# Attention and expert layers on one core: crossbar transposes issued one row further ahead, result stores moved to ScalarE's queue, and a re-ordered start

## The chip, the cores and the metric

The kernel runs on one core of a Trainium2 chip. The metric is the device time in microseconds (us) of one launch. Three runs of the kernel before gave a median of 343.33 us (342.6 to 345.01). Three later sets of rounds gave it medians of 344.21, 345.04 and 346.3 us, so a variant is always compared with runs of the kernel before on the same chip and in the same rounds.

## The reference

Attention with two kinds of heads, followed by a layer of two matrix products with a squared ReLU between:

```python
# q, k, v: (8, 8, 576, 64): batch rows, heads, positions, head size
scores = (q @ k.transpose(0, 1, 3, 2)) / sqrt(64)
rel = pos[:, None] - pos[None, :]
# heads 0..3 ("sliding"): 0 <= rel < 32
# heads 4..7 ("dilated"): 0 <= rel < 128 and rel % 4 == 0
attn = softmax(where(mask, scores, -1e9))
x = (attn @ v).transpose(0, 2, 1, 3).reshape(4608, 512)
h = x @ moe_w_in                 # 512 x 2048
g = maximum(h, 0) ** 2
out = g @ moe_w_out              # 2048 x 512, float32 out
```

## The kernel before

The 4608 tokens are cut in nine chunks of 512. The expert layer of a chunk is 64 matmuls into `ph` (with ReLU on ScalarE and the square on VectorE), then 64 into `po`, each result copied by ScalarE and stored. These are generators. `pump(n)` lets n "steps" of two matmuls each out, and the attention of row b is laid between the steps of chunk b-1. So "row b" and "chunk b-1" name the same stretch of time.

```python
osb   = ctx.enter_context(tc.tile_pool(name="osb", bufs=3))     # relu out and result
pmool = ctx.enter_context(tc.tile_pool(name="pmool", bufs=4, space=PSUM))
# single buffers: QKTp, QKTd (transposed q and k), AT, vp, vd (cast v),
#                 sv, sd (v as loaded), sq (q and k as loaded)

def load_sliding_v(b):               # six DMAs on SP, the sync engine
    for m in range(NB):
        ...
        nc.sync.dma_start(out=sv[p0:P, m, :, :], in_=...)

def load_v(b):
    load_sliding_v(b)
    load_dilated_v(b, nc.sync)       # two more, into sd

def keep_sliding_qk(b, n):           # q, k cast to f16, written to HBM (dd: those of the dilated heads)
    d = dpool.tile([2, S, HH * D], FP16, name=f"dp{b}", tag="dp")
    for i in (1, 0):
        nc.sync.dma_start(out=d[i]..., in_=n[:, i]...)
    return d

def transpose_by_dma(dp, dd):        # the crossbar transposes, T(b) below
    for i in (1, 0):
        nc.sync.dma_start_transpose(out=QKTp[:, i, :, PADP:], in_=dp[i])
        nc.sync.dma_start_transpose(out=QKTd[:, i, :, KPAD:], in_=dd[i])

def store(c, t, po):
    ot = osb.tile([P, DM], FP32, name=f"ot{c}_{t}", tag="ot")
    nc.scalar.copy(ot, po)
    nc.sync.dma_start(out=out[(c*4 + t)*P : (c*4 + t + 1)*P, :], in_=ot)

# ... row 0: on TensorE, alone; row 1: on TensorE, between the steps of chunk 0
for b in range(2, B):
    pending.append(moe_gen(b - 1))
    nq = cast_sliding_qk(b, (nc.gpsimd,) * 4)
    dp = keep_sliding_qk(b, nq)
    transpose_by_dma(dp, dd)         # T(b), for this same row
    cast_v()                         # sv, sd -> vp, vd on GpSimd
    if b + 1 < B:
        load_sliding_qk(b + 1)
        load_v(b + 1)
        dd = keep_dilated_qk(b + 1)
    pump(24)
    attn_scores(b, 4)                # needs T(b)
    attn_values(b, 2)                # needs vp, vd
    pump(1000)
```

Below, v(3) is the v load of row 3, T(3) its transposes, and so on. The "write-out" of a row is its dp.

The softmax here doesn't subtract the row's maximum and nothing guards it: scores larger than these inputs give would overflow.

Of the kernel before, what the change touches and what calls it, by code (L numbers as in the profile page):

```python
# [13 lines left out]
P = 128  # L14
# [3 lines left out]
def kernel(  # L18
# [9 lines left out]
    nc = tc.nc  # L28

    B, H, S, D = q.shape  # L30
# [58 lines left out]
    def load_sliding_qk(b, engs=(nc.sync, nc.sync)):  # L89
        for i, src in enumerate((q, k)):  # L90
            engs[i].dma_start(
                out=sq[:, i, :, :],
                in_=src[b, 0:HH].rearrange("h (p j) d -> p h (j d)", j=6),
            )
# [15 lines left out]
    def load_v(b):  # L110
        load_sliding_v(b)
        load_dilated_v(b, nc.sync)
# [8 lines left out]
                nc.gpsimd.dma_start(out=nd[48 * e : 48 * (e + 1), i, :, :], in_=s4[e])  # L121

    def load_w_in():
        for f0, f1 in ((0, 512), (512, 1024), (1024, 2048)):
            nc.gpsimd.dma_start(
                out=wi[:, :, f0:f1],
                in_=moe_w_in[:, f0:f1].rearrange("(dh dl) f -> dl dh f", dl=P),
            )
# [26 lines left out]
                )  # L155
        return n

    def cast_sliding_v():
        for m in range(0, NB, 2):
            nc.gpsimd.tensor_copy(vp[:, m : m + 2, :, 0:D], sv[:, m : m + 2, :, :])  # L160

    def cast_dilated_v():
        for t in range(2):
            for c in range(0, DIL, 2):
                nc.gpsimd.tensor_copy(  # L165
                    vd[:, t, c : c + 2, :, 0:D],
                    sd[:, t, :, D * c : D * (c + 2)].rearrange("p h (c d) -> p c h d", d=D),
                )
# [29 lines left out]
    load_sliding_qk(0, (nc.sync, nc.scalar))  # L198
    reli = const.tile([P, QB], I16, name="reli")
    nc.gpsimd.iota(reli, pattern=[[1, QB]], base=0, channel_multiplier=-1)  # L200
    make_identity(nc, ident)
    nds = {0: dilated_buffer(0)}
    load_dilated_qk(0, nds[0])
    nc.vector.memset(sv[0:PADP, 0, :, :], 0.0)
    nc.vector.memset(sd[0:64, 0, :, :], 0.0)
    load_sliding_v(0)
    load_dilated_v(0, nc.scalar)
    warm = const.tile([P, 1], FP32, name="warm")
# [63 lines left out]
    def store(c, t, po):  # L272
        ot = osb.tile([P, DM], FP32, name=f"ot{c}_{t}", tag="ot")
        nc.scalar.copy(ot, po)  # L274
        nc.sync.dma_start(out=out[(c * 4 + t) * P : (c * 4 + t + 1) * P, :], in_=ot)

    def mm2_gen(c, g):
        for t in range(TOKC // P):
# [33 lines left out]
    def pump(n):  # L312
        for _ in range(n):
            while pending:
                try:
                    next(pending[0])
                    break
                except StopIteration:
                    pending.pop(0)
# [10 lines left out]
    def t_sliding(b, n, hp, i, wide=False):  # L330
        p_ = pt(f"pt{b}_{hp}_{i}", wide)
        for j in range(6):
            nc.tensor.transpose(
                p_[:, QB * j : QB * (j + 1)],
                n[:, i, j, 2 * hp : 2 * hp + 2, :],
                ident[0:QB, 0:QB],
            )
        copy(
            nc.vector if i else nc.scalar,
            QKTp[:, i, hp, PADP:].rearrange("x (p j) -> x p j", j=6),  # L340
            p_[:, 0:UW].rearrange("x (j p) -> x p j", j=6),
        )

    def t_dilated(b, n, g, i, wide=False):
        p_ = pt(f"pd{b}_{g}_{i}", wide)
        for j in range(6):
            nc.tensor.transpose(
                p_[:, QB * j : QB * (j + 1)],
                n[:, i, g, P * j : P * (j + 1)],
                ident[0:QB, 0:QB],  # L350
            )
        for a in range(2):
            copy(
                nc.vector if i else nc.scalar,
                QKTd[:, i, a, KPAD + 2 * g * CL : KPAD + 2 * (g + 1) * CL].rearrange(
                    "x (h p s) -> x h p s", h=2, s=3
                ),
                p_[:, 0:UW].rearrange("x (s a h p) -> x a h p s", a=2, h=2, p=48)[:, a],
            )
# [5 lines left out]
    def s_sliding(b, hp):  # L365
        tiles = [pa(f"ps{b}_{hp}_{half}") for half in range(2)]
        for half, ps in enumerate(tiles):
            for m3 in range(3):
                m = 3 * half + m3
                for e in range(2):  # L370
                    r = slice(D * e, D * (e + 1))
                    nc.tensor.matmul(  # L372
                        ps[:, e, QB * m3 : QB * (m3 + 1)],
                        QKTp[r, 1, hp, QB * m : QB * m + P],
                        QKTp[r, 0, hp, PADP + QB * m : PADP + QB * (m + 1)],
                        start=True,
                        stop=True,
                    )
        for half, ps in enumerate(tiles):
            softmax(2 * hp + half, ps, maskp)  # L380
# [94 lines left out]
            py[:, 0:UW].rearrange("x (c r i) -> x c i r", c=2, r=DIL),  # L475
        )

    def transposes(b, nq, nd, gap):
        wide = gap == 0
        for hp in range(2):  # L480
            for i in (1, 0):
                t_sliding(b, nq, hp, i, wide)
                pump(gap)
        for g in range(2):
            for i in (1, 0):
                t_dilated(b, nd, g, i, wide and not i)
                pump(gap)

    def attn_scores(b, gap):
        for hp in range(2):  # L490
# [26 lines left out]


    nq = cast_sliding_qk(0, (nc.scalar, nc.scalar, nc.vector, nc.gpsimd))
    cast_sliding_v()  # L520
    load_w_in()
    cast_dilated_v()
    for hp in range(2):
        for i in (1, 0):
            t_sliding(0, nq, hp, i)
        s_sliding(0, hp)
    for g in range(2):
        for i in (1, 0):
            t_dilated(0, nds[0], g, i)
        s_dilated(0, g)  # L530
    attn_values(0, 0)


    g0 = hidden(0)
    pending.append(mm1_gen(0, g0))
    pump(6)
    nds[1] = dilated_buffer(1)
    nc.vector.memset(sq[:, :, :, 0:1], 0.0)
    nc.vector.memset(nds[1][:, :, :, 0:1], 0.0)
    load_sliding_qk(1)  # L540
    load_dilated_qk(1, nds[1])
    load_w_out()
    nq = cast_sliding_qk(1, (nc.gpsimd,) * 4)
    pump(26)
    pending.append(mm2_by_rows_gen(0, g0))
    for hp in range(2):
        for i in (1, 0):
            t_sliding(1, nq, hp, i, True)
            pump(1)
    nc.vector.memset(sv[:, 1, :, 0:1], 0.0)  # L550
    nc.vector.memset(sd[:, 1, :, 0:1], 0.0)
    load_v(1)
    cast_v()
    load_sliding_qk(2)
    load_v(2)
    dd = keep_dilated_qk(2)
    for g in range(2):
        for i in (1, 0):
            t_dilated(1, nds[1], g, i, True)
            pump(1)  # L560
    attn_scores(1, 3)
    attn_values(1, 1, True)
    pump(1000)


    for b in range(2, B):
        pending.append(moe_gen(b - 1))
        nq = cast_sliding_qk(b, (nc.gpsimd,) * 4)
        dp = keep_sliding_qk(b, nq)
        transpose_by_dma(dp, dd)  # L570
        cast_v()
        if b + 1 < B:
            load_sliding_qk(b + 1)
            load_v(b + 1)
            dd = keep_dilated_qk(b + 1)
        pump(24)
        attn_scores(b, 4)
        attn_values(b, 2)
        pump(1000)
    for c in range(B - 1, NTOKC):  # L580
        pending.append(moe_gen(c))
# [31 lines left out]
```

## Time and profile before

| | kernel before |
|---|---|
| time, median of 3 | 343.33 us |
| span of the profiled run | 341.7 us |
| mean granted TensorE clock | 0.99 |
| TensorE busy | 303.1 us (89%) |
| TensorE waits for the transpose of its row | 10.2 us, six waits |
| TensorE waits for a result copy, end of row 1 | 6.6 us, one wait |

Two views carry most of what follows. The waits list says, for an engine and a line of the kernel, what ended the idle time before it, the sum in us, the number of waits and the longest. The slices cut the span in 40 equal parts of 8.5 us, one digit each: busy tenths of an engine, or the granted clock of TensorE. The slices of TensorE in the kernel before:

```profile
PE   0669979938699979998999799979999999999995
PEclk9999999996999999999999999999999999999999
```

After the start there is one deep hole, the 3 in the ninth place, and one slice of low clock behind it. That is the 6.6 us wait at the end of row 1, where ScalarE has no free result buffer because the stores of chunk 0 stand on SP behind other work. The small dips further on are the waits for the transposes of the same row.

### The profile page before, as it was taken

The numbers are of one execution on the slowest core, as the hardware profiler recorded it, in microseconds if no ns is written. First come the engines' busy times: TensorE is split into PE (matmuls) and PEld (weight loads), VectorE is DVE, ScalarE is ACT, GpSimd is POOL, SyncE is SP. The second block draws the span as 40 slices with busy tenths as digits, with TensorE's granted clock in tenths as the row PEclk, the third lists the DMA queues.
The fourth block names the chain that finished last, engine by engine and source line by source line (L and its number), as shares of the span: only waits on it lengthen the run. The fifth ranks groups of instructions, "written<-read, shape, count | busy, mean of one in ns | idle before, by whom it ended". The sixth has DMA issues, their size and how long they took to land.

```text
span 341.7 us, 6096 instructions
## 1 busy us (share of the span) xinstructions
PE 303.1 (89%) x2368; PEld 151.8 (44%) x2368; DVE 155.2 (45%) x354; ACT 171.0 (50%) x292; POOL 74.8 (22%) x119
## 2 busy tenths in 40 slices
PE   0669979938699979998999799979999999999995
PEld 0454434513245434544554355434544554444442
DVE  4574445703475247525743474247525643402400
ACT  2544636305563666367536653656358446514611
POOL 4350632362045003600450054004400000000000
PEclk9999999996999999999999999999999999999999
DMA  8994999987995789479938994799445010011011
GB/s 185 207 157 92 205 210 224 226 235 185 191 209 149 189 179 205 148 195 212 221 123 187 190 211 137 172 181 218 140 132 126 33 61 33 0 61 63 1 53 69
DMA packets 77293, 51.38 MB, mean 150 GB/s; under 512 B 54416, under 2 KB 70800, under 8 KB 77072
## 3 DMA queue, kind: packets, MB, share of 16 engines
q1 hardware_dynamic: 71060, 40.68, 51.4%
q0 software_dynamic: 4976, 8.91, 15.1%
q10 hardware_dynamic: 1228, 1.41, 1.4%
q8 instruction: 18, 0.29, 0.4%
q14 instruction: 11, 0.09, 0.1%
HBM read 39.85 MB, written 16.52 MB: 165 GB/s over the span
## 4 chain that ended last, share of the span: by engine, by line
PE 72%; DMA 18%; DVE 3%; ACT 2%; SPq 1%; POOL 1%; issue 1%; POOLq 0%; ACTq 0%; DVEq 0%
PE po L264 33%; PE ph L249 30%; DMA QKTp<-dp 7%; DMA sq<-in_k_dram 5%; DMA sv<-in_v_dram 5%; PE paw L434 2%; DMA out_dram<-ot 2%; PE ps L372 2%; PE pav L420 2%; PE pz L391 1%; PE px L449 1%; POOL nq L144 1%; ACT AT L362 1%; DVE AT L363 1%; PE py L467 1%
## 5 line engine op out<-in xcount | busy, mean ns | idle before, releaser
L264 PE MATMUL po<-wo,g 128*128 128x512 f16 x576 | 141.3, 379 | 0.0
L249 PE MATMUL ph<-xT,wi 128*128 128x512 f16 x576 | 131.7, 387 | 6.6 <-ACT ot L274 6.6
L260 DVE TENSOR_TENSOR g<-rt 128x512 f16<-128x512 f16 x144 | 61.5, 427 | 109.7 <-ACT rt L259 109.1
L259 ACT ACTIVATE rt<-ph 128x512 f16<-128x512 f32 x144 | 85.9, 598 | 35.6 <-PE ph L249 34.9
L249 PEld LDWEIGHTS <-wi 128*128 128x128 f16 x576 | 56.2, 99 | 75.4 <-issue 11.8
L264 PEld LDWEIGHTS <-g 128*128 128x128 f16 x576 | 49.5, 98 | 45.3
L144 POOL CAST nq<-sq 96x768 f16<-96x768 f32 x29 | 25.0, 903 | 119.4 <-DMA sq<-in_k_dram 119.4
L274 ACT COPY ot<-po 128x512 f32<-128x512 f32 x36 | 21.1, 587 | 59.9 <-PE po L264 51.1
L455 ACT COPY xT<-px 128x576 f16<-128x576 f16 x16 | 10.2, 639 | 29.7 <-PE px L449 29.7
L362 ACT ACTIVATE AT<-ps 128x576 f16<-128x576 f32 x32 | 19.0, 649 | 10.8 <-PE ps L372 10.8
L165 POOL CAST vd<-sd 128x512 f16<-128x512 f32 x32 | 19.5, 620 | 21.9 <-PE paw L434 15.8
L363 DVE TENSOR_TENSOR AT<-AT,maskd 128x576 f16<-128x576 f16 x32 | 19.3, 614 | 10.6 <-ACT AT L362 9.1
L362 ACT ACTIVATE AT<-pz 128x576 f16<-128x576 f32 x32 | 19.0, 649 | 8.0 <-PE pz L391 8.0
L363 DVE TENSOR_TENSOR AT<-AT,maskp 128x576 f16<-128x576 f16 x32 | 15.0, 469 | 16.9 <-ACT AT L362 14.9
L406 DVE TENSOR_TENSOR x_d<-paw,rcp_d 72x512 f16<-72x512 f32 x32 | 22.0, 686 | 1.1
L372 PE MATMUL ps<-QKTp 64*128 64x96 f16 x192 | 7.5, 212 | 12.2 <-DMA QKTp<-dp 10.2
L160 POOL CAST vp<-sv 128x512 f16<-128x512 f32 x24 | 14.4, 626 | 17.3 <-DMA sv<-in_v_dram 17.3
L406 DVE TENSOR_TENSOR x_p<-pav,rcp_p 96x512 f16<-96x512 f32 x24 | 16.5, 686 | 0.8
L434 PEld LDWEIGHTS <-AT 128*128 128x128 f16 x256 | 12.7, 102 | 8.1 <-PE paw L434 1.2
L473 ACT COPY xT<-py 128x576 f16<-128x576 f16 x16 | 10.2, 640 | 10.6 <-PE py L467 10.6
L405 DVE RECIPROCAL rcp_d<-paw 72x8 f32<-72x8 f32 x32 | 6.5, 203 | 19.4 <-PE paw L434 19.3
L434 PE MATMUL paw<-vd,AT 128*128 128x65 f16 x256 | 14.2, 200 | 0.6 <-DVE rcp_d L405 0.4
(54 smaller groups left out, 122.1 us busy)
## 6 DMA issues: line engine op xcount, KB each, us to landing
out_dram<-ot SPq DMA_DIRECT2D x36, 256.0 KB, 2.5
sv<-in_v_dram SPq DMA_DIRECT2D x40, 128.0 KB, 7.2
sq<-in_q_dram SPq DMA_DIRECT2D x8, 576.0 KB, 6.7
sq<-in_k_dram SPq DMA_DIRECT2D x7, 576.0 KB, 7.7
sd<-in_v_dram SPq DMA_DIRECT2D x7, 512.0 KB, 6.3
dp<-nq SPq DMA_DIRECT2D x12, 288.0 KB, 3.5
wo<-in_moe_w_out_dram POOLq DMA_DIRECT2D x4, 512.0 KB, 12.5
sd<-in_v_dram SPq DMA_DIRECT2D x7, 288.0 KB
```

Source lines behind the costliest of these rows:

```text
L144: eng.tensor_copy(o, i)
L160: nc.gpsimd.tensor_copy(vp[:, m : m + 2, :, 0:D], sv[:, m : m + 2, :, :])
L165: nc.gpsimd.tensor_copy(vd[:, t, c : c + 2, :, 0:D], sd[:, t, :, D * c : D * (c + 2)].rearrange("p h (c d) -> p c h d", d=D),)
L249: nc.tensor.matmul(ph, wi[:, dmk, ffc * P : ffc * P + P], xs[:, dmk, :], start=(dmk == 0), stop=(dmk == NDM - 1),)
L259: nc.scalar.activation(rt, ph[:], ACTF.Relu)
L260: nc.vector.tensor_mul(g[:, ffc, :], rt, rt)
L264: nc.tensor.matmul(po, g[:, ffc, t * P : (t + 1) * P], wo[:, ffc, :], start=(ffc == 0), stop=(ffc == NFF - 1),)
L274: nc.scalar.copy(ot, po)
L362: nc.scalar.activation(AT[:, u, 0:UW], ps[:, :, 0 : UW // 2], ACTF.Exp, scale=scale)
L363: nc.vector.tensor_mul(AT[:, u, 0:UW], AT[:, u, 0:UW], mask)
L406: nc.vector.tensor_tensor(out=x[0:w], in0=pv[:, :, :, 0:D], in1=rcp[0:w].unsqueeze(3).to_broadcast([w, 2, HH, D]), op=ALU.mult,)
L434: nc.tensor.matmul(pav[:, e, h * (D + 2) : h * (D + 2) + D + 1], AT[:, 4 + h, off : off + P], vd[:, t, 2 * a + e, h, 0 : D + 1], start=Tru ...
```

## The change

The intent: (1) cast, write out and transpose q and k a whole row before they are used; (2) in rows 0 and 1, let ScalarE make all copies of the transposed q and k of the dilated heads, so that VectorE is free for the masks, and move two memsets to GpSimd; (3) run the first half of row 1's attention (transposes and scores) in one piece, with its v loaded ahead of w_out; (4) issue the result stores from ScalarE, so that SP's order no longer holds them.

```diff
     def store(c, t, po):
         ot = osb.tile([P, DM], FP32, name=f"ot{c}_{t}", tag="ot")
         nc.scalar.copy(ot, po)
-        nc.sync.dma_start(out=out[...], in_=ot)
+        nc.scalar.dma_start(out=out[...], in_=ot)
... (prologue: two memsets from VectorE to GpSimd, w_in in two loads, begin() in place of transposes())
     pending.append(mm1_gen(0, g0))
-    pump(6)
+    pump(4)
...
     load_sliding_qk(1)
+    load_v(1)
     load_dilated_qk(1, nds[1])
+    nq = cast_sliding_qk(1, (nc.gpsimd,) * 4)
     load_w_out()
-    nq = cast_sliding_qk(1, (nc.gpsimd,) * 4)
-    pump(26)
-    pending.append(mm2_by_rows_gen(0, g0))
... (row 1's attention, between steps of mm2)
     cast_v()
     load_sliding_qk(2)
+    dd = keep_dilated_qk(2)
+    nq2 = cast_sliding_qk(2, (nc.gpsimd,) * 4)
     load_v(2)
-    dd = keep_dilated_qk(2)
...
+    dp = keep_sliding_qk(2, nq2)
+    pump(28)
+    begin(1, nq, nds[1])
+    pending.append(mm2_by_rows_gen(0, g0))
+    attn_values(1, 2, True)
     pump(1000)
+    transpose_by_dma(dp, dd)

     for b in range(2, B):
         pending.append(moe_gen(b - 1))
-        nq = cast_sliding_qk(b, (nc.gpsimd,) * 4)
-        dp = keep_sliding_qk(b, nq)
-        transpose_by_dma(dp, dd)
+        pump(1)
         cast_v()
         if b + 1 < B:
-            load_sliding_qk(b + 1)
             load_v(b + 1)
-            dd = keep_dilated_qk(b + 1)
-        pump(24)
+            if b == 2:
+                load_sliding_qk(b + 1)
+                dd = keep_dilated_qk(b + 1)
+            nq = cast_sliding_qk(b + 1, (nc.gpsimd,) * 4)
+            dp = keep_sliding_qk(b + 1, nq)
+            if b + 2 < B:
+                load_sliding_qk(b + 2)
+                dd2 = keep_dilated_qk(b + 2)
+        pump(22 if b == 2 else 2)
         attn_scores(b, 4)
-        attn_values(b, 2)
+        if b + 1 < B:
+            transpose_by_dma(dp, dd)
+            dd = dd2 if b + 2 < B else None
+        attn_values(b, 2 if b == 2 else 3)
         pump(1000)
```

More of the change, by code (lines that the diff above doesn't have):

```diff
@@ L123, in load_w_in @@
     def load_w_in():
-        for f0, f1 in ((0, 512), (512, 1024), (1024, 2048)):
+        for f0, f1 in ((0, 1024), (1024, 2048)):
             nc.gpsimd.dma_start(
@@ L156, in cast_sliding_qk, with cast_sliding_v @@
         return n
-    def cast_sliding_v():
-        for m in range(0, NB, 2):
+    def cast_sliding_v(m0=0, m1=NB):
+        for m in range(m0, m1, 2):
             nc.gpsimd.tensor_copy(vp[:, m : m + 2, :, 0:D], sv[:, m : m + 2, :, :])
@@ L200 @@
     nc.gpsimd.iota(reli, pattern=[[1, QB]], base=0, channel_multiplier=-1)
-    make_identity(nc, ident)
+    nc.gpsimd.memset(sv[0:PADP, 0, :, :], 0.0)
+    nc.gpsimd.memset(sd[0:64, 0, :, :], 0.0)
     nds = {0: dilated_buffer(0)}
     load_dilated_qk(0, nds[0])
-    nc.vector.memset(sv[0:PADP, 0, :, :], 0.0)
-    nc.vector.memset(sd[0:64, 0, :, :], 0.0)
+    make_identity(nc, ident)
     load_sliding_v(0)
@@ L274, in store @@
         nc.scalar.copy(ot, po)
-        nc.sync.dma_start(out=out[(c * 4 + t) * P : (c * 4 + t + 1) * P, :], in_=ot)
+        nc.scalar.dma_start(out=out[(c * 4 + t) * P : (c * 4 + t + 1) * P, :], in_=ot)
     def mm2_gen(c, g):
@@ L342, in t_sliding, with t_dilated @@
         )
-    def t_dilated(b, n, g, i, wide=False):
+    def t_dilated(b, n, g, i, wide=False, eng=None):
         p_ = pt(f"pd{b}_{g}_{i}", wide)
@@ L353, in t_dilated @@
             copy(
-                nc.vector if i else nc.scalar,
+                eng or (nc.vector if i else nc.scalar),
                 QKTd[:, i, a, KPAD + 2 * g * CL : KPAD + 2 * (g + 1) * CL].rearrange(
@@ L476, in x_dilated, with begin @@
         )
-    def transposes(b, nq, nd, gap):
-        wide = gap == 0
+    def begin(b, nq, nd):
         for hp in range(2):
             for i in (1, 0):
-                t_sliding(b, nq, hp, i, wide)
-                pump(gap)
+                t_sliding(b, nq, hp, i)
         for g in range(2):
+            s_sliding(b, g)
             for i in (1, 0):
-                t_dilated(b, nd, g, i, wide and not i)
-                pump(gap)
+                t_dilated(b, nd, g, i, eng=nc.scalar)
+        for g in range(2):
+            s_dilated(b, g)
     def attn_scores(b, gap):
@@ L519 @@
     nq = cast_sliding_qk(0, (nc.scalar, nc.scalar, nc.vector, nc.gpsimd))
-    cast_sliding_v()
+    cast_sliding_v(0, 2)
     load_w_in()
+    cast_sliding_v(2, NB)
     cast_dilated_v()
-    for hp in range(2):
-        for i in (1, 0):
-            t_sliding(0, nq, hp, i)
-        s_sliding(0, hp)
-    for g in range(2):
-        for i in (1, 0):
-            t_dilated(0, nds[0], g, i)
-        s_dilated(0, g)
+    begin(0, nq, nds[0])
     attn_values(0, 0)
@@ L540 @@
     load_sliding_qk(1)
+    load_v(1)
     load_dilated_qk(1, nds[1])
+    nq = cast_sliding_qk(1, (nc.gpsimd,) * 4)
     load_w_out()
-    nq = cast_sliding_qk(1, (nc.gpsimd,) * 4)
-    pump(26)
-    pending.append(mm2_by_rows_gen(0, g0))
-    for hp in range(2):
-        for i in (1, 0):
-            t_sliding(1, nq, hp, i, True)
-            pump(1)
-    nc.vector.memset(sv[:, 1, :, 0:1], 0.0)
-    nc.vector.memset(sd[:, 1, :, 0:1], 0.0)
-    load_v(1)
     cast_v()
     load_sliding_qk(2)
+    dd = keep_dilated_qk(2)
+    nq2 = cast_sliding_qk(2, (nc.gpsimd,) * 4)
     load_v(2)
-    dd = keep_dilated_qk(2)
-    for g in range(2):
-        for i in (1, 0):
-            t_dilated(1, nds[1], g, i, True)
-            pump(1)
-    attn_scores(1, 3)
-    attn_values(1, 1, True)
+    dp = keep_sliding_qk(2, nq2)
[3 more added lines that the diff above has]
+    attn_values(1, 2, True)
     pump(1000)
+    transpose_by_dma(dp, dd)
     for b in range(2, B):
         pending.append(moe_gen(b - 1))
-        nq = cast_sliding_qk(b, (nc.gpsimd,) * 4)
-        dp = keep_sliding_qk(b, nq)
-        transpose_by_dma(dp, dd)
+        pump(1)
         cast_v()
         if b + 1 < B:
-            load_sliding_qk(b + 1)
             load_v(b + 1)
-            dd = keep_dilated_qk(b + 1)
-        pump(24)
+            if b == 2:
[7 more added lines that the diff above has]
+        pump(22 if b == 2 else 2)
         attn_scores(b, 4)
-        attn_values(b, 2)
+        if b + 1 < B:
+            transpose_by_dma(dp, dd)
+            dd = dd2 if b + 2 < B else None
+        attn_values(b, 2 if b == 2 else 3)
         pump(1000)
```

## The prediction

> **What bounds the kernel now.** I read, in this order, the page's busy table, the time slices, the waits of TensorE, the chain that ended last in order of time, the waits of the SP queue, and busy time in windows cut at the row borders.
>
> The busy table says who is near the limit:
>
> ```profile
> PE 303.1 (89%) x2368; PEld 151.8 (44%) x2368; DVE 155.2 (45%) x354; ACT 171.0 (50%) x292; POOL 74.8 (22%) x119
> ```
>
> TensorE is busy for 303 of 341.7 us; no other engine passes 50%. Only its gaps can be won, 38.6 us in all. The waits of TensorE name them (engine, line, what it waited for, us in total, times, longest):
>
> ```profile
> PE ps L372 <- DMA QKTp<-dp: 10.2, 6, 3.0
> PE pt L333 <- DVE nq L144: 9.2, 1, 9.2
> PE ph L249 <- ACT ot L274: 6.6, 1, 6.6
> PE pz L391 <- DVE QKTd L144: 2.4, 2, 1.5
> PE pt L333 <- POOL nq L144: 2.3, 3, 1.2
> ```
>
> The 9.2 us are the first load and its cast, which the change leaves alone. The 10.2 us are six waits, one in each of rows 2 to 7, for the crossbar transpose of that same row. The 6.6 us are one wait, at the end of row 1, for ScalarE to empty an accumulator. The windows (stretch, length, busy us of each engine, clock, DMA share, GB/s) for rows 2, 3 and 7 and the last two token chunks:
>
> ```profile
> 78.38:113.40 35.02, 32.02 (x256) 15.57 (x256) 17.55 (x38) 17.85 (x31) 9.58 (x15) 0.94 0.88 186
> 113.40:147.70 34.30, 32.45 (x270) 16.30 (x269) 17.15 (x38) 18.81 (x32) 8.66 (x13) 1.00 0.77 181
> ...
> 250.20:282.90 32.70, 32.45 (x269) 16.28 (x268) 16.71 (x38) 18.77 (x32) 0.00 (x0) 1.00 0.32 88
> 282.90:341.70 58.80, 55.20 (x256) 24.85 (x254) 13.61 (x32) 24.40 (x41) 0.00 (x0) 1.00 0.11 41
> ```
>
> A row with next to no wait (row 7) takes 32.7 us with 32.45 busy; that is the floor of a row. The tail is pure matmul and 58.8 us. The chain shows how the 6.6 us arose:
>
> ```profile
> 55.87 1.10 SPq L91
> 57.55 12.02 DMA sv<-in_v_dram
> 70.68 1.10 SPq L108
> 71.87 5.77 DMA out_dram<-ot
> 78.38 9.31 PE ph L249 x32
> ```
>
> The stores of chunk 0 stand on SP's queue behind the v loads of row 2, which wait for casts. The first store goes out at 71.87, ScalarE waits for its three-deep result buffer, TensorE for ScalarE. SP's own waits say the same: stores wait, but mostly because they are early.
>
> **What the Trainium skill says.** "DMA: Bandwidth & Descriptors", section "Issuing engines are not separate DMA queues": all issuers share the same 16 DMA engines. Moving stores to ScalarE therefore buys queue order, no bandwidth; the trace agrees so far as DMA is near full (the slices of 34 to 85 us read 7 to 9 tenths or more). The same page, "Anatomy of one DMA": a semaphore wait is served on the issuing sequencer ahead of dispatch. In this trace SP stood so while loads waited for casts; after the change ScalarE itself stands so at each store. "TensorE: Matmul & The Clock Gate", "Part 1: The HAM clock gate": a cold array issues 512-column matmuls every 427 ns, a warm one every 216 ns. The trace agrees: 13.81 us for 64 in the tail is 216 ns, and from 78.38, after the 6.6 us stall, they come every 0.42 us until 82.98. That costs about (82.98 - 78.38) / 0.42 = 11 matmuls times 0.21, or 2.2 us.
>
> **The change, part by part.**
>
> (1) *Transposes one row ahead.* The transposes for row b+1 now follow the scores of row b, with the values stage and the end of the row (some 22 us) to land in. They take 3.6 us each to land and four issues of 1.3 to 1.6 us, about 10 us in sequence. What they need (q and k loaded, cast, written out) comes earlier on SP and GpSimd, whose casts are 3.6 + 4.4 = 8 us a row. This removes the 10.2 us of waits. Moving the scores to the start of a row (3 steps in, not 24) puts their exps beside the ReLUs: a group of scores then holds TensorE for 0.43 + 8 x 0.216 = 2.16 us and ScalarE for 1.19 + 2 x 0.60 = 2.39 us. The 0.23 us lag per group is mostly swallowed by the four accumulators; I charge 0.2 us a row, 1 us in all.
>
> (2) *First row's evacuations.* Now two copies of 0.76 on VectorE, on ScalarE two of 0.64, eight of 0.35 and four pairs of exps (1.19 us a pair): 1.3 + 2.8 + 4.8 = 8.9 us of ScalarE, back to back from the first transposes' end near 10.3. Scores end near 19.9 and the masks on VectorE near 20.5; before, the first reciprocal came at 22.30. Gain 1.7 us, carried unchanged through seven normalisations of 0.9 us. The first expert matmul moves from 28.9 to about 27.2. Issue of w_in moves from 17.0 to about 14, early enough for this.
>
> (3) *Row 1.* Loads leave after 4 steps, not 6, near 31.6 (before 34.25). q and k land in about 8 us, casts of 4 x 0.83 end near 43; mm1 of chunk 0 ends near 27.2 + 13.8 + 1.5 (cold) = 42.5. The first half of row 1's attention then runs bare, without matmuls between, for the same 9 us of ScalarE, to 52; values and mm2 take 13.8 + 4.8 us more, to about 71. So TensorE alone would be done with row 1 about 4 us earlier than before (68.8 + 6.6 of stall).
>
> (4) *Stores through ScalarE.* SP's order no longer holds them. But the wait list of the changed program, as built, shows what does. DMA completion semaphores are dealt in turn from eight, over SP and ScalarE together, and a DMA waits for the last user of its semaphore. The stores of chunk 0 wait for a transpose of row 2 and for pieces 0, 1 and 3 of the v load of **row 3**. Those follow on SP: q, k of row 2 land near 54, cast to 58, written out near 59 and landed near 65, four transposes issued to 70, v pieces from 70 with 7 us to landing (median in the trace 7.3): near 78.5. ScalarE stands at the stores until then, its ReLUs behind it, and TensorE stalls again after two of its four accumulators. It resumes half cold near 76.6 and is back in step as if chunk 1 had begun at 77.0. Before, the same count was 78.38 - 12 x 0.216 + 2.2 = 78.0. So the 6.6 us stall is not removed, it changes its cause; parts 2 to 4 together give only 1 us. In rows 3 to 6 I find no such loss: the first store comes 21 us into a row and the transpose it waits for lands at about 17; the later ones wait for v pieces that land 3 us ahead or just in time. At the end of row 2 the last store waits for a v piece of row 4 to land near 113, against a start of row 3 at 110; accumulators cover most of it. I charge 1 us.
>
> *The sum*, on the profile's span: 77.0 + 6 x 32.45 + 1 (exps) + 1 (row 2) + 0.5 (other) + 58.8 = 333.0. The same sum for before is 78.0 + 194.7 + 10.2 + 58.8 = 341.7, its span. Timed runs lie 1.6 us over the span (343.33 against 341.7): **334.6**, rounded 334.5, 2.6% faster.
>
> **Rivals.** *A: the stores do not stall ScalarE* (the v pieces of row 3 land by 71, or copies go first). For it: DMA has slack at 15 to 20 us and 30 to 40 us (shares 0.36 and 0.48) that earlier loads can fill. Against it: weights, three rows of loads and one of transposes must pass by then at near full DMA. Chunk 1 then counts from 71, the span is about 71 + 194.7 + 2.5 + 58.8 = 327 and the time 328.5. *B: DMA becomes the bound of the first 80 us.* The queue table charges 15.1% to GpSimd's queue and 51.4% to SP's, 227 us of full DMA for 51 MB; about a third of this has to pass ahead of those stores. If w_out, now behind row 1's casts, comes late, mm2 waits, and v of row 3 lands at 85 or later: 340 or so. *C: ScalarE's blocked stores recur in every row* because a transpose or v piece lands late. At 2 us a row it gives back the 10.2 us: about 345. Against it, my slack of 3 to 4 us in rows 3 to 6. *D: transposes hidden and nothing else changed:* 343.3 - 10.2 = 333, near my number for another reason; the traces tell them apart by the start of chunk 1.
>
> **Range and chances.** The 10.2 us are well founded. What varies is when chunk 1 starts (71 to 83) and up to 4 us of new waits later. Hence 327 to 341 for 8 in 10, the middle just beyond the 2% mark (336.5): faster 0.70, same 0.27, slower 0.03.
>
> **What would show it.** Right: no wait of scores for the transpose; rows 3 to 7 at 32.5 to 33 us; first expert matmul near 27; ScalarE waiting at stores of chunk 0 for v loads, to 75 to 82 us, with TensorE waiting there for ScalarE. Wrong: chunk 1 running smoothly from 71 (too slow a prediction), mm2 waiting for w_out, or ScalarE waiting 2 us or more at stores of chunks 2 to 5 (too fast a one).

## The result, and the profile after

The changed kernel took 355.46 us (median of 3 runs, 355.34 to 356.65). The ratio to the kernel before is 1.0354, with a 95% interval of 1.0285 to 1.0423: slower. A ratio here is the mean time of one kernel's fast runs over that of the other's fast runs of the same rounds, so it isn't quite the ratio of the medians. Executions over 1.5% slower than the fastest of the same kernel are left out of the means. The time is outside the predicted range of 327 to 341 us, on the side that had a chance of 0.03.

The start of the first expert matmul of each chunk, read from the traces, shows where the time went. The last two lines give how long each chunk took:

| us | chunk 0 | 1 | 2 | 3 | 4 | 5 | 6 | 7 | span |
|---|---|---|---|---|---|---|---|---|---|
| before, start | 28.9 | 69.0 | 113.4 | 147.7 | 181.0 | 215.3 | 250.0 | 282.7 | 341.7 |
| after, start | 28.3 | 77.7 | 128.5 | 166.3 | 198.7 | 231.0 | 263.3 | 295.7 | 354.7 |
| after less before | -0.6 | 8.7 | 15.1 | 18.6 | 17.7 | 15.7 | 13.3 | 13.0 | 13.0 |
| before, length | 40.1 | 44.4 | 34.3 | 33.3 | 34.3 | 34.8 | 32.7 | 59.0 (7, 8) | |
| after, length | 49.4 | 50.8 | 37.8 | 32.3 | 32.3 | 32.3 | 32.3 | 59.0 (7, 8) | |

Chunks 3 to 6 became as short as a chunk can be (TensorE has no wait in them): the gain that was wanted is there, 5.6 us over these four. Chunks 0, 1 and 2 lose 9.3, 6.4 and 3.5 us. The busy table, the slices of TensorE, and then three of its waits, after the change:

```profile
PE 311.1 (88%) x2368; PEld 155.8 (44%) x2368; DVE 151.4 (43%) x342; ACT 168.9 (48%) x300; POOL 78.7 (22%) x120
PE   0769955982699786999999999999999999999995
PEclk9999985895699988999999999999999999999999
```

```profile
PE ph L249 <- ACT ot L274: 11.0, 2, 8.1
PE po L264 <- DMA wo<-in_moe_w_out_dram: 3.2, 1, 3.2
PE py L467 <- ACT xT L455: 3.2, 1, 3.2
```

From the 17th slice on, the row of nines has no dip. The waits for the transpose are gone from the list. But the hole at the end of row 1 is deeper (2 and 6 in place of 3 and 8), and there are new dips and low clock ahead of it. TensorE does the same 2368 matmuls in 8.0 us more of busy time, as more of them run at the lower clock (the mean granted clock is 0.952, before 0.990). The wait for ScalarE's result copy grew from 6.6 to 11.0 us.

What ScalarE did in that hole is the core of the case. Its timeline gives start, duration, the engine or its DMA queue, what it did, and in brackets the idle time before and what ended it:

```profile
75.28 0.59 ACT L274 COPY ot<-po 128x512 f32<-128x512 f32 x1 [1.95 <-PE po L264]
85.75 0.38 ACTq L275 DMA_DIRECT2D out_dram<-ot  x1
86.17 0.59 ACT L274 COPY ot<-po 128x512 f32<-128x512 f32 x1 [10.30 <-DMA QKTd<-dd]
90.48 0.36 ACTq L275 DMA_DIRECT2D out_dram<-ot  x1
90.88 0.59 ACT L274 COPY ot<-po 128x512 f32<-128x512 f32 x1 [4.12 <-DMA sv<-in_v_dram]
...
93.03 1.57 ACT L259 ACTIVATE rt<-ph 128x512 f16<-128x512 f32 x3 [0.47 <-ACT ot L274]
```

The first result is copied at 75.28 and its buffer is ready at 75.87, but its store is issued only at 85.75. In between ScalarE does nothing. What ended the wait is a *transpose of row 2's k*, which has nothing to do with that result: it landed at 85.67. The second store waits likewise for a piece of v(3). In the built program the four stores of chunk 0 wait for the completion semaphores of this transpose and of the first, second and fourth piece of v(3), in this order. Not until 93.03 does ScalarE come to the ReLUs of chunk 1, and TensorE has only four accumulators to run ahead with.

Why are those transfers so late? SP's timeline:

```profile
50.21 12.98 SPq L100 DMA_DIRECT2D sv<-in_v_dram  x6
63.29 5.09 SPq L107 DMA_DIRECT2D sd<-in_v_dram  x1
...
70.12 1.58 SPq L186 DMA_DIRECT2D dp<-nq  x2
77.33 1.50 SPq L194 DMA_TRANSPOSE QKTp<-dp  x1
...
86.29 3.76 SPq L100 DMA_DIRECT2D sv<-in_v_dram  x6
```

The row "dp" is the write-out of row 2's cast q and k. GpSimd had these ready at 61.4 (its four casts start at 58.28 and take 3.15 us), but SP was then issuing v(2), and the issue itself was slow: 12.98 us for six pieces, 5.09 us for one more. So the write-out went at 70.12 and its first half landed at 77.25, T(2) was issued from 77.33 to 86.2, and v(3) from 86.29.

The same stretches as windows (stretch, length, busy us of TensorE, weight loads, VectorE, ScalarE, GpSimd with their counts, granted clock, DMA share, GB/s):

```profile
28.30:77.70 49.40, 41.87 (x321) 21.44 (x319) 22.38 (x42) 21.38 (x40) 22.26 (x33) 0.86 0.93 191
77.70:91.50 13.80, 2.86 (x9) 0.92 (x8) 0.00 (x0) 1.17 (x2) 0.76 (x2) 0.64 1.04 199
91.50:128.50 37.00, 33.83 (x260) 16.10 (x260) 18.30 (x38) 18.27 (x32) 13.11 (x19) 0.92 0.89 210
128.50:166.30 37.80, 34.51 (x269) 16.82 (x268) 16.15 (x38) 18.15 (x32) 9.01 (x13) 0.95 0.88 212
166.30:198.70 32.40, 32.40 (x270) 16.21 (x269) 16.15 (x38) 18.15 (x32) 9.00 (x13) 1.00 0.87 189
```

In chunk 0 (first line) TensorE is busy for 41.87 us; for the same stretch of the kernel before, 28.9 to 69.0, that view gives 37.61 us at a clock of 1.00. So 4.3 us of the 9.3 lost in chunk 0 are slower matmuls, and 5.0 us are more waiting. In the second line the core all but stands: 2.86 us of work in 13.8.

### The profile page after: what moved, and what is told of

Read it like the earlier page. It is cut to its first block, busy times and chain, and to the rows that moved or that the text cites. A ratio compares the mean times of both kernels' runs of the same rounds, so it can differ in the third digit from the quotient of the medians.

```text
span 354.7 us, 6082 instructions
## 1 busy us (share of the span) xinstructions
PE 311.1 (88%) x2368; PEld 155.8 (44%) x2368; DVE 151.4 (43%) x342; ACT 168.9 (48%) x300; POOL 78.7 (22%) x120
## 4 chain that ended last, share of the span: by engine, by line
PE 76%; DMA 11%; SPq 5%; ACT 3%; DVE 2%; issue 1%; POOL 1%; ACTq 0%; POOLq 0%
PE po L264 35%; PE ph L249 33%; DMA sv<-in_v_dram 5%; DMA wo<-in_moe_w_out_dram 3%; SPq L100 2%; PE paw L434 2%; DMA sq<-in_k_dram 2%; PE pav L420 2%; PE px L449 1%; SPq L195 1%; PE pz L391 1%; ACT AT L362 1%; PE ps L372 1%; PE py L467 1%; SPq L194 1%
## 5 line engine op out<-in xcount | busy, mean ns | idle before, releaser
L249 PE MATMUL ph<-xT,wi 128*128 128x512 f16 x576 | 141.2, 394 | 11.0 <-ACT ot L274 11.0
L264 PE MATMUL po<-wo,g 128*128 128x512 f16 x576 | 138.2, 387 | 3.2 <-DMA wo<-in_moe_w_out_dram 3.2
L260 DVE TENSOR_TENSOR g<-rt 128x512 f16<-128x512 f16 x144 | 64.7, 452 | 138.4 <-ACT rt L259 136.3
L259 ACT ACTIVATE rt<-ph 128x512 f16<-128x512 f32 x144 | 83.8, 602 | 38.7 <-PE ph L249 32.2
L249 PEld LDWEIGHTS <-wi 128*128 128x128 f16 x576 | 54.5, 101 | 74.9 <-issue 21.2
L264 PEld LDWEIGHTS <-g 128*128 128x128 f16 x576 | 53.6, 99 | 60.6 <-issue 6.2
L160 POOL CAST vp<-sv 128x512 f16<-128x512 f32 x24 | 17.1, 722 | 94.6 <-issue 49.5
L363 DVE TENSOR_TENSOR AT<-AT,maskp 128x576 f16<-128x576 f16 x32 | 18.3, 578 | 5.8 <-ACT AT L362 4.0
L363 DVE TENSOR_TENSOR AT<-AT,maskd 128x576 f16<-128x576 f16 x32 | 15.3, 492 | 5.4 <-ACT AT L362 4.4
L333 PE MATMUL pt<-ident,nq 96*128 96x96 f16 x48 | 4.0, 243 | 12.3 <-DVE nq L144 9.1
```

The costliest lines, as they stand in the source:

```text
L160: nc.gpsimd.tensor_copy(vp[:, m : m + 2, :, 0:D], sv[:, m : m + 2, :, :])
L249: nc.tensor.matmul(ph, wi[:, dmk, ffc * P : ffc * P + P], xs[:, dmk, :], start=(dmk == 0), stop=(dmk == NDM - 1),)
L259: nc.scalar.activation(rt, ph[:], ACTF.Relu)
L260: nc.vector.tensor_mul(g[:, ffc, :], rt, rt)
L264: nc.tensor.matmul(po, g[:, ffc, t * P : (t + 1) * P], wo[:, ffc, :], start=(ffc == 0), stop=(ffc == NFF - 1),)
L363: nc.vector.tensor_mul(AT[:, u, 0:UW], AT[:, u, 0:UW], mask)
```

## The experiments

Twelve kernels were run, all correct. Shared semaphores need one sentence of background that the built programs show: each DMA issued by SP or ScalarE signals its end on one of eight semaphores, dealt in turn in the order of the whole program, and before it is issued it waits for the previous user of its own. "Lane" below means such a semaphore.

### Whose queue the stores are on

**e1: the changed kernel with one line put back.**

```diff
-        nc.scalar.dma_start(out=out[...], in_=ot)
+        nc.sync.dma_start(out=out[...], in_=ot)
```

> The changed kernel with one word undone: results leave through SP's queue again, as before the change. Theory A (ScalarE stands at each store, because the store waits for the completion semaphore that a v load or a transpose of a later row used last): the 11.0 us wait of the chunk matmuls for the result copy and the 3.2 us wait of the last transposes of row 2 fall to 3 us or less together, row 3 comes down from 38.0 to under 35 us, and the time falls to 338 to 344. Rival B (the first 90 us are bound by DMA, whichever queue stores use): the transposes of row 2 still land near 89 us, scores of row 2 wait for them instead, and the time stays at 350 or more.

Measured: 344.49 us (343.69 to 348.22), ratio 1.0061 [0.999, 1.0133]; the kernel before had 344.21 us on this chip. One line accounts for the slowdown against the kernel before, yet nothing of the hoped-for gain appears. The wait for the result copy is gone from TensorE's list, and this came instead:

```profile
PE ps L372 <- DMA QKTp<-dp: 9.8, 2, 8.2
```

Nearly all of it is one wait, in row 3: the row begins at 111.6, its scores now come after 3 steps, and T(3) landed only at 121.2.

**f0: stores on ScalarE, but with lanes that are free.** This keeps the stores where the change put them. Chunk 1 is begun, and two tiny memsets hold T(2) until its first square is done, so that in the program's order the stores of chunks 0 and 1 come before the transfers that they had to wait for.

```diff
     pump(1000)
+    pending.append(moe_gen(1))
+    pump(2)
+    nc.vector.memset(QKTp[:, :, :, PADP : PADP + 2], 0.0)
+    nc.vector.memset(QKTd[:, :, :, KPAD : KPAD + 2], 0.0)
     transpose_by_dma(dp, dd)
```

> The changed kernel, stores still on ScalarE's queue, but the transposes of row 2 (and all that stands behind them on SP) are held until the first squared tile of chunk 1 exists. In the built wait list this puts the stores of chunks 0 and 1 ahead of them, so these eight stores wait only for the semaphores of transfers that landed long before; the order of ScalarE is otherwise the same. Theory A (the shared completion semaphores make the stall): ScalarE waits for no v load and no transpose up to row 3, the 11.0 + 3.2 us waits of TensorE go, a wait of the scores for the transposes comes in their place as in the run with SP's queue, time 341 to 347. If the cost is ScalarE's issuing itself (36 issues of 0.35 us on its queue), the time stays at 352 or more.

Measured: 346.87 us (346.68 to 348.54), ratio 1.007 [1.0021, 1.0119]. Chunk 1 took 33.7 us (77.2 to 110.9) in place of 50.8, and ScalarE stands at no store for more than 0.3 us. So it isn't the store on ScalarE as such that costs the time, but what the store has to wait for. As f0 also moves those transfers later, it alone can't tell a shared semaphore from another kind of wait for them; the waits in the built program and the issue at 85.75, right after the landing at 85.67, do. Then, as in e1, row 3 waits for its transpose:

```profile
PE ps L372 <- DMA QKTp<-dp: 11.6, 2, 10.3
```

**e3: the kernel before with only the stores moved.**

```diff
-        nc.sync.dma_start(out=out[...], in_=ot)
+        nc.scalar.dma_start(out=out[...], in_=ot)
```

> The kernel before with one word changed: results leave through ScalarE's queue, nothing else. Theory A: in its wait list the third store of a chunk waits for a transpose of the next row, which is issued only in that next row, so ScalarE stands some 10 us in each of rows 2 to 6: 370 us or more, with TensorE waiting for ScalarE. The view that moving stores off SP's blocked queue is a gain in itself: the 6.6 us wait at the end of row 1 goes and the time is 335 to 341.

Measured: 347.3 us (345.92 to 350.46), ratio 1.0135 [1.0065, 1.0205], unclear by the 2% verdict. The size was missed: I had expected some 10 us in every row. One long stall came, 13.5 us of ScalarE waiting for a v piece at the last store of chunk 1; at one store of each of chunks 1 to 4 ScalarE stood 1.2 to 2.4 us, which didn't lengthen chunks 3 and 4. Each of chunks 3 to 6 took 32.3 to 32.4 us, although the program of this kernel issues T(b) in row b (33.3, 34.3, 34.8 and 32.7 before). So what chunks 3 to 6 gain in the changed kernel can be had from the store's queue alone. The traces show why. Before, T(5) is issued from 185.84, behind the stores of chunk 3 on SP, when row 5 has already begun (181.0). In e3 it is issued from 173.34, 19 us before its row begins at 192.6: without stores, SP runs on into the next row by itself, and T(3) to T(7) all go a row ahead. The two parts of the change aim at the same waits, and their gains can't be added.

**e2: the changed kernel with its stores on GpSimd.**

```diff
-        nc.scalar.dma_start(out=out[...], in_=ot)
+        nc.gpsimd.dma_start(out=out[...], in_=ot)
```

> The changed kernel with results leaving through GpSimd's queue, whose completion semaphores are not those of SP and ScalarE. Theory A: ScalarE is freed here too, so the time is as in the run with SP's queue within 4 us (338 to 346); GpSimd's casts of v are put off behind the stores but have slack. Rival B: 350 or more. If this one is fast and the one on SP's queue is not, SP's order matters and not the semaphores.

Measured: 367.21 us (364.36 to 368.22), ratio 1.0689 [1.0622, 1.0755]. The expectation was missed: the lanes shared with SP are gone (row 3 waits 9.8 us for T(3), as in e1), and a new cost takes their place. Chunks 3 to 5 took 37.8 to 38.4 us. GpSimd stood with the last store at each row's end (issued at 196.01 here), and then did all its casts in one go at the start of the next row. Its timeline there, then VectorE's:

```profile
196.55 1.72 POOL L160 CAST vp<-sv 128x512 f16<-128x512 f32 x3
198.22 2.28 POOL L165 CAST vd<-sd 128x512 f16<-128x512 f32 x4
200.45 3.13 POOL L144 CAST nq<-sq 96x768 f16<-96x768 f32 x4
```

```profile
196.58 7.28 DVE L260 TENSOR_TENSOR g<-rt 128x512 f16<-128x512 f16 x1 [10.16 <-ACT rt L259]
```

One square on VectorE took 7.28 us, about as long as the eleven casts beside it, which run from 196.55 to 203.58; a square with no cast beside it takes 0.42 us. The Trainium skill, "SBUF — State Buffer", section "SBUF: two separate sides", says that VectorE and GpSimd share a pair of ports under an exclusive lock, and that a VectorE operation with two inputs in SBUF takes part in it. The trace agrees with such a lock, and looks as if it were held over eleven instructions in a row.

### What is needed besides

**e4: the kernel before through row 1, then the loop of the changed kernel, stores on SP.** This asks what "one row ahead" alone is worth.

```diff
+    nq2 = cast_sliding_qk(2, (nc.gpsimd,) * 4)     # within row 1
+    dp = keep_sliding_qk(2, nq2)
...
+    transpose_by_dma(dp, dd)                       # ahead of the loop
... (loop of the changed kernel)
```

> The kernel before through row 1, with only the transposes one row ahead (the loop of the changed kernel, q and k of row 2 cast and written out in row 1), stores on SP's queue. If the transposes ahead are worth what the waits say (10.2 us over rows 2 to 7, of which the wait of row 2 is least sure), the time is 333 to 337 and rows 3 to 7 take 32.3 to 33 us each. If they are worth nothing without the rest of the change, 342 to 345.

Measured: 344.86 us (344.22 to 345.31), ratio 1.0045 [0.9988, 1.0101]: the same as before. Chunks 3 to 6 took 32.3 us each, but scores waited 9.1 us for transposes (8.3 in one) and TensorE 4.9 us for a result copy. To be a row ahead in the later rows, the kernel has to gain that row once, and in rows 2 and 3 that costs what the later rows give back.

**f1: e1, with row 3's scores moved back to step 22 of the row.**

```diff
-        pump(22 if b == 2 else 2)
+        pump(22 if b <= 3 else 2)
         attn_scores(b, 4)
...
-        attn_values(b, 2 if b == 2 else 3)
+        attn_values(b, 2 if b <= 3 else 3)
```

> The run with stores on SP's queue, and row 3 keeps its scores 23 steps into the row as row 2 does, not 3. There the 8.2 us wait in row 3 was for transposes that landed at 121 us, 9 us after the row began. If the DMA is simply not yet a row ahead at row 3, the wait of row 3 falls under 1 us, rows 4 to 7 stay at 32.3 us, and the time is 334 to 338 (344.5 less 8.2 is 336.3). If the wait only moves to row 4, 342 or more.

Measured: 345.63 us (345.31 to 346.06), ratio 1.0028 [0.9976, 1.008]. A miss, and a telling one. The wait for the transpose fell from 9.8 to 1.7 us, and as much came back elsewhere:

```profile
PE ph L249 <- ACT ot L274: 9.6, 1, 9.6
PE ps L372 <- DMA QKTp<-dp: 1.7, 1, 1.7
```

The four stores of chunk 1 now stand on SP behind T(3) (issued 108.4 to 120.0), ScalarE has three result buffers, and TensorE waits for it.

**g2: f1 with six result buffers in a pool of their own.**

```diff
+    otp = ctx.enter_context(tc.tile_pool(name="otp", bufs=6))
...
-        ot = osb.tile([P, DM], FP32, name=f"ot{c}_{t}", tag="ot")
+        ot = otp.tile([P, DM], FP32, name=f"ot{c}_{t}", tag="ot")
```

> f1 (stores on SP, row 3's scores at step 22) with only one thing of f2: six result buffers in place of three. f1 took 345.6 and f2, with buffers and order, 331.4. Theory (both matter: buffers remove the 9.6 us wait of TensorE for the result copy, order removes the late transposes of rows 2 and 3): 336 to 341, with no wait for the result copy over 1 us and a wait of scores for the transpose of 1 to 5 us. Rival X (the order alone carries it; the wait only moves): 344 to 347. Rival Y (the buffers alone carry it): 331 to 333.

Measured: 337.15 us (336.07 to 338.78), ratio 0.9768 [0.971, 0.9825], as expected: faster, though the interval leaves the 2% verdict unclear. The result copy is gone from the list of waits, and scores wait 4.2 us for two transposes.

**f2: g2 with another order on SP.** The write-out and transposes of row 2 go ahead of v(2), and q, k of row 3 ahead of v(3).

```diff
-    load_v(2)
     dp = keep_sliding_qk(2, nq2)
     pump(28)
     begin(1, nq, nds[1])
+    transpose_by_dma(dp, dd)
+    load_v(2)
+    load_sliding_qk(3)
     pending.append(mm2_by_rows_gen(0, g0))
     attn_values(1, 2, True)
     pump(1000)
-    transpose_by_dma(dp, dd)
...
             load_v(b + 1)
             if b == 2:
-                load_sliding_qk(b + 1)
                 dd = keep_dilated_qk(b + 1)
```

> As the run with the late scores of row 3, and on SP's queue the q and k of row 2 are written out and transposed ahead of the load of v of row 2, q and k of row 3 are loaded ahead of v of row 3, and results have six buffers of their own. In the run on SP's queue the issue of the v loads kept SP until 70 us, so q and k, cast at 61, went out at 70 and the transposes landed at 89. Theory C (order on SP, not the bytes, makes row 2's transposes late): they land by 76 to 80 us, scores of row 2 wait under 1 us, time 331 to 336. If the bytes bind (DMA full from 34 to 90 us), something else of row 2, v or the stores, is late instead and the time is within 2 us of the run with late scores.

Measured: 331.39 us (330.95 to 331.93), ratio 0.9611 [0.9568, 0.9654]. This beats both kernels. Every chunk from 1 to 6 took 32.3 to 32.4 us. SP's timeline, against that of the changed kernel above:

```profile
59.95 1.87 SPq L187 DMA_DIRECT2D dp<-nq  x2
67.29 2.30 SPq L195 DMA_TRANSPOSE QKTp<-dp  x1
...
74.78 3.29 SPq L101 DMA_DIRECT2D sv<-in_v_dram  x6
```

The write-out goes at 59.95 rather than 70.12, and T(2) is issued from 67.29 to 74.7 rather than to 86.2. The six v pieces then take 3.29 us to issue, not 12.98. The bytes are the same; it was the order that made T(2) late. Slow issues aren't gone: v(3)'s six pieces take 11.97 us, from 83.81, but what stands behind them has more time, T(3) being issued to 114.4 for scores that come 23 steps into a row begun at 109.3.

### The pieces of f2, taken apart

**g3: f2 with the stores back on ScalarE's queue,** one line.

```diff
-        nc.sync.dma_start(out=out[...], in_=ot)
+        nc.scalar.dma_start(out=out[...], in_=ot)
```

> f2 with one line altered: stores back on ScalarE's queue. Semaphores shared as in g1. Theory (a store on ScalarE stands for a foreign transfer whatever the number of buffers): ScalarE waits at the stores of chunk 0 for v of row 2 until 80 to 85 and at the last of chunk 1 for v of row 4; 331.4 plus 6 to 12: 337 to 344. Rival (with six buffers and the good order the queue of the stores is indifferent): 330 to 333.

Measured: 346.75 us (345.84 to 350.36), ratio 1.0049 [0.998, 1.0118]. With everything else as in the best version, the store's queue alone costs 346.75 - 331.39 = 15 us, though the two ran in different rounds of the same chip (the ratios, 1.0049 and 0.9611, say the same: 4.4% of 345 us). The direction was as expected, the size larger. ScalarE's timeline near the end of chunk 1:

```profile
103.71 0.59 ACT L275 COPY ot<-po 128x512 f32<-128x512 f32 x1
119.43 0.34 ACTq L276 DMA_DIRECT2D out_dram<-ot  x1
119.81 0.64 ACT L456 COPY xT<-px 128x576 f16<-128x576 f16 x1 [15.51 <-DMA QKTd<-dd]
```

A result that was ready at 104.3 leaves at 119.43, and behind it stands the copy that TensorE needs for row 2's attention. Six buffers don't help: it isn't a buffer that is missing, it is the engine that stands.

**g1: the changed kernel with only the order of f2** (stores on ScalarE, three buffers, scores of row 3 early; the edit is f2's second diff alone).

> The changed kernel (stores on ScalarE's queue, three result buffers) with only the order on SP altered: written-out q and k of row 2 and their transposes ahead of the v load of row 2, and q, k of row 3 ahead of the v load of row 3. As built, the four stores of chunk 0 then share their semaphores with pieces 1, 2, 4 and 5 of the v load of row 2, not of row 3. Theory (the order on SP made the releasing transfers late): transposes of row 2 issued 67 to 75, those v pieces landed by 80 to 85, so chunk 1 counts from about 83 instead of 91.6; the loss at the last store of chunk 1 (5 us, v of row 4) stays. 355.5 less 8 to 11: 344 to 348. Rival (the bytes, not the order: DMA is full up to 90 us): the pieces land at 90 all the same, 352 or more.

Measured: 346.85 us (344.11 to 348.61), ratio 1.0025 [0.9959, 1.0091]. The time was as expected, the path to it wasn't. At the stores of chunk 0 ScalarE now waited 3.7 us for v(2), and TensorE waited 3.0 us for result copies in place of 11.0. But the second store of chunk 1 now stood 13.3 us for T(3), where I had expected 5 us at the last one. So the order on SP is confirmed as what made chunk 0's stores late, and the stall comes back at whatever store of the next chunk shares a lane with a late transfer.

**f4: f2 with row 1 laid between the steps of chunk 0, as in the kernel before,** and w_out loaded ahead of v(1).

```diff
     load_sliding_qk(1)
-    load_v(1)
     load_dilated_qk(1, nds[1])
-    nq = cast_sliding_qk(1, (nc.gpsimd,) * 4)
     load_w_out()
+    load_v(1)
+    nq = cast_sliding_qk(1, (nc.gpsimd,) * 4)
... (begin(1) replaced by row 1's pieces with pump(1) and pump(3) between)
```

> As the run before it, and row 1 as in the kernel before the change: transposes and scores of row 1 between matmuls of chunk 0 and not bare, w_out loaded ahead of v of row 1. In the changed kernel row 1 was 9.2 us longer (chunk 1 began at 77.7 us against 69.0). If that is the bare stretch and the late w_out, chunk 1 begins at 69 to 71 us and the time is 323 to 329; if DMA binds there too, chunk 1 begins early but waits for the transposes of row 2, and the time is 330 or more.

Measured: 334.58 us (334.02 to 335.3), ratio 0.9704 [0.9661, 0.9748]. Chunk 0 took 40.7 us in place of f2's 48.8, so the new form of row 1 is what loses 8 to 9 us there. But q and k of row 2 then came later on SP (written out at 70.14, in f2 at 59.95), scores waited 9.4 us for transposes, and chunks 2 and 3 took 40.8 and 34.1 us. The new form of row 1 costs 8 us and buys the time to get ahead. Which of the two edits in f4 made chunk 0 short and row 2's q and k late, w_out or the interleaving, was not separated.

**g4: f4 with row 3's transposes ahead of v(3) as well, and one prologue load moved from ScalarE to SP.**

```diff
-    load_dilated_v(0, nc.scalar)
+    load_dilated_v(0, nc.sync)
... (in the loop, for b == 2 only:)
+            nq = cast_sliding_qk(b + 1, ...)       # ahead of cast_v()
+            dp = keep_sliding_qk(b + 1, nq)
+            cast_v()
...
             transpose_by_dma(dp, dd)
+            load_v(b + 1)                          # behind T(b + 1)
```

> f4 (row 1 interleaved as in the kernel before, six buffers, stores on SP) with row 3's casts, write-out and transposes ahead of the v load of row 3 too, and the first dilated v load on SP rather than ScalarE. In f4 row 3 still waited 7.1 us for its transpose and rows 2 and 3 took 10 us over 32.3. Theory (row 3's transposes stand behind 13 us of v pieces on SP): that wait falls under 2 us, chunk 2 begins near 102 and every later row takes 32.3 to 33; 323 to 329. First expert matmul 1 to 2 us sooner (near 27). Rival (GpSimd's casts at the start of row 2, beside VectorE's squares, cost as much as in e2, some 5 us in that row): 329 to 334.

Measured: 341.13 us (339.02 to 342.97), ratio 0.9865 [0.9802, 0.9928]. A miss. The cast of v(2) now stands on GpSimd behind a cast of q and k of row 3 that waits for its load until 94.77, and row 2's values wait for it (scores also wait 6.6 us for transposes):

```profile
PE pav L421 <- POOL vp L161: 7.5, 1, 7.5
```

The prologue part did what was said: the first expert matmul came at 27.0, in f4 at 28.3. f2 stays the best version that was run.

## Why the prediction was wrong

**The bound, and parts (1) and (2).** The first steps held. The waits of scores for the transposes are gone, and chunks 3 to 6 took 32.3 us, slightly better than the 32.5 to 33 that were said. The charge of 1 us for exps beside ReLUs was not needed there: in those chunks TensorE is busy for the whole length. Row 0 gained 0.6 us, not 1.7. The term that failed is ScalarE's start: the working has its copies begin near 10.3, and they began at 12.65. The first dilated v load is issued from ScalarE at 8.16 (before: 2.23), with ScalarE's casts of q behind it (10.59, before 7.48). The memset that this load needs had ended at 2.18; in the built program it also waits for the semaphore of the first load of k, whose cast on GpSimd starts at 8.14. So this is the shared semaphore again. With that load on SP (g4) the casts start at 7.74 and the first expert matmul came at 27.0 against the predicted 27.2.

**Part (3), row 1, failed.** It was to end near 71, and it ended at 77.7. The sum took a clock of 1.0 nearly throughout and w_out in time. Measured were a clock of 0.86 (41.87 us busy, where the kernel before has 37.61), and 5.0 us more waiting, 3.2 of it for w_out. That last was in rival B's text and should have been in the sum: the change puts w_out behind row 1's casts. In this run the stand at the stores covers it; f2 still carries it (chunk 1 begins at 77.0).

**Part (4), the stores, had the right mechanism and the wrong size.** It named the shared semaphores, the transposes of row 2 and the pieces of v(3); the trace shows ScalarE standing for exactly these. The release was put at 78.5; the last of those v pieces landed at 92.0, and the last store left at 92.6. This is some 14 of the 21.7 us by which the span missed the sum (354.7 against 333.0). The mis-sized term is the chain on SP. The working had the write-out at 59, because the cast ends by then, and took 1.3 to 1.6 us for an issue. It left out that SP had v(2)'s eight loads ahead of it, and that these were slow to issue: 50.2 to 70.0 (the DMA share was 1.18 from 50.2 to 63.2; whether that is why was not tested). From there everything is 11 to 16 us late: T(2) issued to 86.2 rather than 70, v(3) from 86.29. g1 against the changed kernel, and f2 against g2, confirm the term: with only the order changed, the write-out goes at 59.91 and 59.95, where the prediction had it.

**The loss in later rows was under-charged.** "I charge 1 us" at the end of row 2 was 5.05 us of ScalarE at the last store of chunk 1, for v(4), after 7.9 us at an earlier store of that chunk for a transpose, of which 3.2 us reached TensorE. Chunk 2 took 37.8 us where a later one takes 32.3. The prediction's sign of a wrong sum, ScalarE waiting 2 us or more at stores of chunks 2 to 5, did not come: from chunk 2 on every store leaves 0.03 us after its copy. The waits were one chunk earlier. g1 and g3 show how fragile this is: move the transfers, and the stall moves to another store, 13.3 or 15.5 us long.

**The rivals.** Rival B had the right row (w_out late, v of row 3 late, "340 or so") and named DMA's bytes as the cause. For v and the transposes f2 and g1 show the order to be the cause, as the bytes are the same; for w_out bytes stay possible (TensorE waits 2.8 us for it in f2 too). Rival C, a stall in every row, fell: the stores of chunks 0 and 1 stand, no later one does. The deeper fault of the prediction is that it gave one store's wait as a date, 78.5, and a range of 71 to 83 round it, though it rested on a chain of eight loads, a write-out and four transposes. An error in such a chain is likely one-sided: a link left out can only make it later.

**Where the expected gain went.** Being a row ahead must be earned once, and in later rows it comes with the stores' queue alone (e3). Rows 1 to 3 have to move one extra row's q and k through a DMA system that is near full (share 0.93 and 1.04 in the windows). With stores on SP this comes out even (e1, e4); with stores on ScalarE the lateness is handed to ScalarE, and so to TensorE, which costs 10 us more (355.46 against 344.49 us; ratios 1.0354 and 1.0061). With the better order and six result buffers it comes out 3.9% ahead (f2).

## What to carry to other kernels

A store that is moved to a compute engine's queue stops that engine until the store may be issued, and it may have to wait for a foreign transfer that shares its completion semaphore. Read in the built program what each store waits for, and follow *that* transfer back through its queue before counting on the move. On a queue that issues in order, put the transfers with a long chain behind them (write-out, then transpose) ahead of bulk loads, and give results enough buffers that a late store costs nothing.

## What the Trainium skill lacked or had wrong

- "DMA: Bandwidth & Descriptors", section "Issuing engines are not separate DMA queues", says that issuing from several engines saves only the time on the sequencer. Here the choice of the issuer alone cost 15 us (g3 against f2), as ScalarE stood 15.51 us at one store. The same page's "Anatomy of one DMA" has the wait on the issuing sequencer, which the traces agree with; no page read says what completion semaphores shared between two issuers cost in time, when one waits for the other's transfers (10.30 us for a transpose, 4.12 us for a v piece in the changed kernel).
- That section calls the issue of a DMA usually small relative to the DMA itself. In the changed kernel one load's issue held SP for 5.09 us and six took 12.98 us; in f2 the six of the same row, issued behind T(2), took 3.29 us. The page gives no figure for an issue that is held up like this, and no run here shows what it waits for.
- "SBUF — State Buffer", section "SBUF: two separate sides", gives the lock as held for the whole instruction. In e2 one square was kept for 7.28 us, over eleven GpSimd casts in a row, and this recurred: three of the 48 squares from 156 to 270 us took 7.28 us each. How long a chain of instructions can keep the pair is not stated.
